# Retention and MLP on one core: splitting a mask, moving a cast, and swapping two loads in a queue

## The chip, the cores and the metric

The kernel runs on one core of one Trainium2 chip. The metric is the device time of one execution in microseconds (us), lower is better. Most executions of one kernel agree within about 0.3%, some 0.6 us here, and that turned out to be as large as everything that this change does. The chip's time is about 1.8 us longer than the span of the profile throughout: in the changed kernel, 215.22 us goes with a span of 213.4 us. Spans and moments inside the trace are used to find causes, repeated times to give verdicts.

## The reference, cut to what matters

A retention recurrence over 4 sequences of 768 steps with 8 heads of 64, then layer norm and an MLP of 512 to 2048 to 512 with a residual:

```python
for t in range(S):
    state = gamma * state + einsum('bhd,bhe->bhde', k[:, :, t], v[:, :, t])
    y[:, :, t] = scale * einsum('bhd,bhde->bhe', q[:, :, t], state)
...
x  = y, heads side by side: [4, 768, 512]
xn = (x - mean) / sqrt(var + 1e-6) * g_ln
out = x + relu(xn @ w_ch1) @ w_ch2
```

## The kernel before

The rows are cut into 24 tiles of 128. For each tile the recurrence is done in chunked form: k and q are transposed, for tiles 0 to 6 on TensorE (the code calls these steps tk and tq) and for later ones by DMA; the scores are a product `pa`, masked and evacuated to `asb` on VectorE, and the output `py` is `asb` by v plus q by the state. `pd` updates the state. Layer norm gives `xn`, which is transposed (tx; from tile 8 on by DMA), and the MLP follows. A unit of the first MLP matmul is 16 small matmuls: in the early groups, one tile by one quarter of `w1`, 0.89 us of TensorE. Up to a planned 14 us, gaps of TensorE are filled with matmuls of zeros, so not all of its busy time there is work.

The instruction order is not written by hand. Every step is a task with its durations, a rank and its inputs. A greedy planner simulates the engines and emits the tasks in the order that it finds:

```python
def order(self):
    ...
    while any(todo.values()):
        ...            # of all tasks that could start: the smallest (start + polite, rank, start)
        at = max(free[e], t["at"], ring[-self.depth] if t["load"] else 0)
        ...
        key = at + t["polite"], t["rank"], at
        if best is None or key < best[0]:
            best = key, t, e
```

So a changed constant of one task can move many others. The parts that the change touches are the mask of the scores, the casts of tile 0 (which alone arrives as fp32, by other queues), and the ranked list of loads that GpSimd issues:

```python
maskd = a(DVE, 1230, -50, c_mask, [vscd, tri])          # one 128 x 1024 product
...
loaded[kind, j] = a({"k": {ACT: 620}, "q": {DVE: 490}, "v": {ACT: 620, DVE: 430}}[kind], 0, -60, emit,
                    [raw], takes, [("osb", kind)])      # tile 0: v goes to either engine
...
first = ["iota", "pos", "k1", "q1", "v1", "w1_0", "k2", "q2", "w1_1", "v2", "k3", "q3", "v3",
         "w1_2", "k4", "q4", "v4", "w1_3", "k5", "q5", "v5"]
```

`w1_2` is the third of four quarters of the first weight, counted from 0. In the texts of the prediction and the experiments it is "quarter 3 of w1", and tiles are counted from 0.

## Time and profile before

| | before |
|---|---|
| time, median of 3 | 214.69 us (214.67 to 214.78) |
| span of the profiled execution | 213.1 us |
| TensorE busy | 203.6 us, 96% |
| first `pa` (scores of tile 0) starts | 7.69 us |
| first MLP unit starts | 13.69 us |
| k of tile 4 has landed, its transposes start | 23.34, 23.38 us |
| k of tile 6 has landed, its transposes start | 31.29, 32.75 us |
| second MLP matmul starts | 48.18 us |
| last matmul starts | 209.80 us |

Moments in tables and text are read from single records and can differ by 0.01 from the rows shown, by rounding. Reading it: TensorE has no long gap after the first 24 us, so the question for any early change is which of its early waits ends last. The prediction reads that out of the views. It does not show VectorE (DVE) at the head, which is what the change is about. In these rows of VectorE's timeline of the kernel before, the columns are start, duration, engine, line, operation, output and inputs, shapes, count, and in brackets the idle time ahead of the row with what ended it:

```profile
4.36 1.23 DVE L262 TENSOR_TENSOR mask<-vsc,cm 128x1024 f32<-128x1024 f32 x1
5.60 0.49 DVE L188 CAST qsb<-osb 128x512 bf16<-128x512 f32 x1
6.88 0.43 DVE L188 CAST v<-osb 128x512 bf16<-128x512 f32 x1 [0.79 <-DMA osb<-in_v_dram]
7.22 0.42 DVE L416 TENSOR_TENSOR trq<-tp,qsc 128x512 bf16<-128x512 bf16 x1
```

VectorE does the whole mask, casts q, then stands 0.79 us for the raw v, casts it, and only then scales the transposed q, on which the first `pa` waits. A chain of three small costs sits ahead of the first scores.

### The profile page before, as it was taken

How to read it: one execution, taken by the hardware profiler on the slowest of the kernel's cores; microseconds unless marked ns; L12 is line 12 of the kernel's file. 1: busy time of each engine (PE TensorE's matmuls, PEld its weight loads, DVE VectorE, ACT ScalarE, POOL GpSimd, SP SyncE). 2: the span in 40 equal slices, each digit the busy share in tenths (PEclk: the TensorE clock that was granted, in tenths of full speed). 3: DMA queues.
4: the chain of work that ended last, by engine and by line, in shares of the span. 5: the costliest groups of instructions: out<-in, count | busy, mean ns of one | idle time of the engine just before them, and what ended most of it. 6: DMA issues, size and time to landing. Idle time of an engine off the chain costs nothing.

```text
span 213.1 us, 4678 instructions
## 1 busy us (share of the span) xinstructions
PE 203.6 (96%) x1935; PEld 131.4 (62%) x1955; DVE 121.3 (57%) x235; ACT 80.8 (38%) x152; POOL 89.8 (42%) x105
## 2 busy tenths in 40 slices
PE   7769999999999999999999999999999999999994
PEld 2448899995476556777877785454544444444442
DVE  7688778961736989987872869793511111012121
ACT  4446655772042203645644353145640044430000
POOL 8988699826498395665834550000000000000000
PEclk9999999999999999999999999999999999999999
DMA  7999999999999999999999999820121111011212
GB/s 140 180 179 180 180 156 190 169 185 155 149 202 190 130 245 201 134 165 128 172 131 142 122 177 152 222 77 0 34 65 50 52 49 49 0 52 49 98 49 98
DMA packets 109382, 27.17 MB, mean 127 GB/s; under 512 B 102065, under 2 KB 106417, under 8 KB 109362
## 3 DMA queue, kind: packets, MB, share of 16 engines
q0 software_dynamic: 75984, 13.24, 87.8%
q1 hardware_dynamic: 32194, 13.31, 34.7%
q10 hardware_dynamic: 1184, 0.33, 0.7%
q8 instruction: 15, 0.25, 0.5%
q14 instruction: 5, 0.04, 0.1%
HBM read 27.27 MB, written 6.29 MB: 157 GB/s over the span
## 4 chain that ended last, share of the span: by engine, by line
PE 87%; DMA 8%; POOL 2%; issue 1%; DVE 0%; POOLq 0%
PE tp L626 39%; PE mm L589 37%; DMA ksb<-in_k_dram 5%; DMA w<-in_moe_w_ch_dram 3%; PE pa L443 3%; PE pd L512 2%; PE py L466 2%; PE py L462 2%; PE tp L542 1%; POOL k L342 0%; PE tp L403 0%; POOL qsb L342 0%; POOL v L342 0%; POOL w L350 0%; PE tp L411 0%
## 5 line engine op out<-in xcount | busy, mean ns | idle before, releaser
L589 PE MATMUL mm<-xnt,w 128*128 128x128 bf16 (+2 forms) x896 | 93.7, 257 | 0.0
L626 PE MATMUL tp<-w,h 128*128 128x512 bf16 (+2 forms) x381 | 86.7, 370 | 1.2 <-issue 0.3
L602 ACT ACTIVATE h<-mm 128x512 bf16<-128x512 f32 x88 | 52.5, 597 | 70.5 <-PE mm L589 59.6
L589 PEld LDWEIGHTS <-w 128*128 128x128 bf16 x896 | 65.7, 98 | 18.5
L626 PEld LDWEIGHTS <-h 128*128 128x128 bf16 x400 | 37.3, 98 | 38.8
L634 DVE SCALAR_TENSOR_TENSOR osb<-tp,rstd,x_all 128x512 f32<-128x512 f32 (+2 forms) x25 | 18.2, 728 | 55.3 <-PE tp L626 55.1
L450 DVE TENSOR_TENSOR asb<-pa,mask 128x1024 bf16<-128x1024 f32 x24 | 29.3, 1220 | 9.6 <-PE pa L443 9.4
L480 DVE BATCH_NORM_STATS2 bns<-py 128x6 f32<-128x512 f32 x24 | 16.7, 696 | 14.6 <-PE py L466 14.4
L499 POOL TENSOR_TENSOR vg<-vsb,vsc 128x512 bf16<-128x512 bf16 x16 | 17.2, 1073 | 13.3 <-DMA vsb<-in_v_dram 9.2
L486 ACT CAST x_all<-py 128x512 bf16<-128x512 f32 x24 | 14.0, 583 | 19.1 <-DVE xn L475 19.0
L342 POOL DMA_DIRECT2D qk<-in_k_dram x17 | 15.2, 893 | 12.3 <-DMA tr<-qk 9.9
L342 POOL DMA_DIRECT2D vsb<-in_v_dram x20 | 18.5, 923 | 1.2 <-DMA w<-in_moe_w_ch_dram 0.8
L475 DVE SCALAR_TENSOR_TENSOR xn<-py,mv,gb 128x512 bf16<-128x512 f32 x24 | 18.0, 751 | 0.9
L526 DVE TENSOR_TENSOR state<-pd,gch 64x256 bf16<-64x256 f32 x40 | 16.7, 417 | 0.3
L342 POOL DMA_DIRECT2D qk<-in_q_dram x17 | 15.2, 894 | 3.4 <-DMA w<-in_moe_w_ch_dram 3.4
L433 DVE TENSOR_TENSOR trq<-tr,qsc 128x512 bf16<-128x512 bf16 x17 | 7.9, 463 | 2.9 <-DMA tr<-qk 2.9
L564 ACT ACTIVATE rstd<-mv,epsb 128x1 f32<-128x1 f32 (+2 forms) x14 | 3.7, 289 | 11.8 <-DVE mv L481 11.8
L466 PEld LDWEIGHTS <-asb 128*128 128x128 bf16 x192 | 7.8, 98 | 0.3 <-DVE trq L416 0.3
L462 PEld LDWEIGHTS <-trq 128*128 128x128 bf16 x80 | 6.0, 98 | 3.2
L466 PE MATMUL py<-vsb,asb 128*128 128x64 bf16 x160 | 7.9, 193 | 0.0
L462 PE MATMUL py<-state,trq 128*128 128x128 bf16 x80 | 7.7, 219 | 0.1
L650 PE MATMUL mm<-zeros 128*128 128x512 bf16 (+1 forms) x24 | 6.4, 394 | 1.4 <-DVE zeros L221 1.2
(65 smaller groups left out, 108.4 us busy)
## 6 DMA issues: line engine op xcount, KB each, us to landing
out_dram<-osb SPq DMA_DIRECT2D x23, 256.0 KB, 4.0
w<-in_moe_w_ch_dram POOLq DMA_DIRECT2D x8, 512.0 KB, 10.3
vsb<-in_v_dram POOLq DMA_DIRECT2D x20, 128.0 KB, 8.8
qk<-in_k_dram POOLq DMA_DIRECT2D x17, 128.0 KB, 9.3
qk<-in_q_dram POOLq DMA_DIRECT2D x17, 128.0 KB, 9.9
qsb<-in_q_dram POOLq DMA_DIRECT2D x6, 128.0 KB, 8.7
k<-in_k_dram POOLq DMA_DIRECT2D x3, 128.0 KB, 7.4
v<-in_v_dram POOLq DMA_DIRECT2D x3, 128.0 KB, 9.0
```

The costliest lines, as they stand in the source:

```text
L342: nc.gpsimd.dma_start(out=tile_of(kind, j), in_=src)
L450: nc.vector.tensor_tensor(out=take("asb", t, [P, NPAIR, 2, P], BF16).rearrange("p i a t -> p a i t"), in0=held["pa", t], in1=mask.rearrang ...
L462: nc.tensor.matmul(py[:, 2 * i:2 * i + 2, :], lhsT=held["trq", t][:, i, :], rhs=held["pb", t][:, i, :], start=(mi == 0), stop=False)
L466: nc.tensor.matmul(py[:, h, :], lhsT=held["asb", t][:, h // 2, h % 2, :], rhs=tile_of("v", t)[:, h, :], start=(mi == 0), stop=(mi == n - 1))
L475: nc.vector.scalar_tensor_tensor(out=take("xn", t, [P, DM], BF16), in0=held["py", t].rearrange("p h d -> p (h d)"), scalar=mv[:, t, 0:1], ...
L480: nc.vector.bn_stats(out=bns[:, t, :], in_=held["py", t].rearrange("p h d -> p (h d)"))
L499: e.tensor_tensor(out=take("vg", j, [P, H, D], BF16), in0=tile_of("v", j), in1=vsc[:, cc, :].unsqueeze(2).to_broadcast([P, H, D]), op=ALU. ...
L526: nc.vector.tensor_tensor(out=held["pb", n][o, :, o], in0=held["pd", b][o, :, o], in1=gch[o, cc, :].unsqueeze(2).to_broadcast([D, NPAIR, D ...
L589: nc.tensor.matmul(p[:, j, :], lhsT=w1[:, ko, (ho + j) * P:(ho + j + 1) * P], rhs=held["xnt", hb][:, h0:h0 + n, ko, :], start=(ko == 0), s ...
L602: nc.scalar.activation(out=dst, in_=src, func=AF.Relu)
L626: nc.tensor.matmul(held[key], lhsT=held["h1", hb][:, ho, i * P:(i + 1) * P], rhs=w2[:, ho, cols], start=(ho == 0), stop=(ho == HO - 1))
L634: nc.vector.scalar_tensor_tensor(out=take("osb", key, [P, w], FP32), in0=held[key], scalar=rstd[:, t:t + 1], in1=x_all[:, t, cols], op0=AL ...
```

## The change

The intent is to start earlier: cut the mask in two so that half of it fills VectorE's idle time, give the cast of v to ScalarE, and put weights and v where the new, earlier TensorE order asks for them. Several cost constants of the planner are changed with it, so its whole early order shifts.

```diff
--- before.py
+++ after.py
@@ -258,10 +258,11 @@
         nc.vector.tensor_scalar(out=cm, in0=fidx, scalar1=pos[:, 0, 0:1], scalar2=None,
                                 op0=ALU.is_ge)
 
-    def c_mask(eng):
+    def c_mask(eng, s):
+        n = s.stop - s.start
         nc.vector.tensor_tensor(
-            out=mask, in0=vsc[:, 0, :].unsqueeze(2).to_broadcast([P, H, P]),
-            in1=cm.unsqueeze(1).to_broadcast([P, H, P]), op=ALU.mult)
+            out=mask[:, s], in0=vsc[:, 0, s].unsqueeze(2).to_broadcast([P, n, P]),
+            in1=cm.unsqueeze(1).to_broadcast([P, n, P]), op=ALU.mult)
 
     def c_gch(eng):
         for c in range(1, C):
@@ -272,7 +273,7 @@
             nc.gpsimd.memset(x, 0.0)
 
     a = plan.add
-    small = a(DVE, 1450, -100, c_small)
+    small = a(DVE, 1550, -100, c_small)
     small2 = a(DVE, 200, -99, c_small2)
     iota = a(POOL, 250, 0, c_iota)
     ipos = a(POOL, 250, 0, c_pos)
@@ -285,7 +286,9 @@
     table = a(ACT, 1300, -100, lambda eng: None)
     vscd = a(ACT, 250, -90, c_vsc, [lmul, table])
     qscd = a(ACT, 700, -91, c_qsc, [args, table])
-    maskd = a(DVE, 1230, -50, c_mask, [vscd, tri])
+
+    maskd = a(DVE, 640, -50, lambda eng: c_mask(eng, slice(0, H // 2)), [vscd, tri])
+    maskd = a(DVE, 640, -45, lambda eng: c_mask(eng, slice(H // 2, H)), [maskd], at=5300)
     gchd = a(ACT, 900, 100, c_gch, [small, qscd, vscd], at=9000)
     zerod = a(POOL, 500, 0, c_zero, at=9000)
     exps = [gchd, qscd, vscd]
@@ -327,12 +330,12 @@
                     dst = take("osb", kind, [P, DM], FP32).rearrange("p (h d) -> p h d", d=D)
                     (nc.scalar if eng == ACT else nc.sync).dma_start(out=dst, in_=src)
                 raw = a(ACT if kind == "q" else SP, 390, -200 + "kqv".index(kind), emit32, (),
-                        ("osb", kind), (), 0, {"k": 3400, "q": 4000, "v": 4800}[kind])
+                        ("osb", kind), (), 0, {"k": 3400, "q": 3800, "v": 5200}[kind])
 
                 def emit(eng):
                     evacuate(eng, take(*takes, [P, H, D], BF16),
                              held["osb", kind].rearrange("p (h d) -> p h d", d=D))
-                loaded[kind, j] = a({"k": {ACT: 620}, "q": {DVE: 490}, "v": {ACT: 620, DVE: 430}}[kind], 0, -60, emit,
+                loaded[kind, j] = a({"k": {ACT: 620}, "q": {DVE: 490}, "v": {ACT: 620}}[kind], 0, -60, emit,
                                     [raw], takes, [("osb", kind)])
                 return
 
@@ -349,15 +352,15 @@
             def emit(eng):
                 nc.gpsimd.dma_start(out=dst, in_=src)
         loaded[kind, j] = a(POOL, ns, rank, emit, (), takes, uses, dma,
-                            4000 if kind in "qkv" and j > 7 else 1400 if late(kind, j) else 500,
+                            4000 if kind in "qkv" and j > 7 else 1400 if late(kind, j) else 900 if kind == "w1" and j else 500,
                             follows=follows)
 
     def late(kind, j):
-        return j > 2 if kind in "qkv" else kind == "w2" or j > 0
-
-
-    first = ["iota", "pos", "k1", "q1", "v1", "w1_0", "k2", "q2", "w1_1", "v2", "k3", "q3", "v3",
-             "w1_2", "k4", "q4", "v4", "w1_3", "k5", "q5", "v5"]
+        return j > 2 if kind in "qkv" else kind == "w2" or j > 1
+
+
+    first = ["iota", "pos", "k1", "q1", "v1", "w1_0", "k2", "q2", "w1_1", "v2", "k3", "q3", "w1_2",
+             "v3", "k4", "v4", "q4", "w1_3", "k5", "v5", "q5"]
     pool_rank = {x: i - 1000 for i, x in enumerate(first)}
     seq = [(x, t) for t in range(8) for x in "kqv"] + [("w1", j) for j in range(4)]
     seq += [("w2", j) for j in range(4)] + [(x, 8) for x in "kqv"]
@@ -516,7 +519,7 @@
                 pdt = a(PE, 230, r - 1 if cc == 0 else r + 2.2, e_pd,
                         [vgt, loaded["k", j]] + ([pbt[j]] if cc else []),
                         ("pd", b) if cc == 0 else None,
-                        [("vg", j), where["k", j]] + ([("pd", b)] if cc else []), at=0 if cc or b else 20000)
+                        [("vg", j), where["k", j]] + ([("pd", b)] if cc else []), at=0 if cc or b else 19000)
 
                 def e_pb(eng, n=number[b, cc + 1], b=b, cc=cc):
```

> **What bounds the kernel now.** I first read the page's busy line and its chain of shares. They say that TensorE (PE) is the bound, with one stretch of DMA in the chain.
>
> ```profile
> PE 203.6 (96%) x1935; PEld 131.4 (62%) x1955; DVE 121.3 (57%) x235; ACT 80.8 (38%) x152; POOL 89.8 (42%) x105
> PE 87%; DMA 8%; POOL 2%; issue 1%; DVE 0%; POOLq 0%
> ```
>
> The busy line hides when PE is free, so I read the waits of PE next. Each row is who waited for whom, total us, times, longest.
>
> ```profile
> PE pa L443 <- DVE trq L416: 1.1, 2, 0.6
> PE mm L542 <- DVE xn L475: 0.7, 1, 0.7
> PE tp L542 <- DVE xn L475: 0.7, 1, 0.7
> ...
> PE tp L403 <- DMA ksb<-in_k_dram: 0.4, 1, 0.4
> ```
>
> There are few, and the timeline dates them: 12.18, 15.76, 20.42 us and, last of all, 23.39 us. The chain that ended last, asked for the first 30 us in order of time (start, us, what), shows what that last one is.
>
> ```profile
> 4.19 7.25 DMA w<-in_moe_w_ch_dram
> 11.45 0.28 issue
> 11.73 0.76 POOL w L350
> 12.49 0.17 issue
> 12.66 10.68 DMA ksb<-in_k_dram
> 23.34 0.05 issue
> 23.39 0.40 PE tp L403 x4
> 23.78 0.89 PE mm L589 x16
> 24.68 0.22 PE tp L411 x4
> 24.90 0.89 PE mm L589 x16
> ```
>
> The reader is to see a hand-over. Up to 23.34 us the end is set by a load: k of tile 4, issued at 12.66 and landed 10.68 us later, because it stands in a queue of loads. From 23.39 us on there is only PE, back to back, to the end of the span (213.1 us). So the time is **the start of the transposes of k of tile 4, plus 189.7 us of PE work** (213.1 - 23.39). Gaps of PE before 23.39 us cost nothing by themselves: whatever PE gains there, it waits away at that load.
>
> The timeline of PE around that point shows how the wait is filled today:
>
> ```profile
> 20.42 0.40 PE L443 MATMUL pa<-trq,trk 64*128 64x128 bf16 x8 [0.44 <-DVE trq L416]
> 20.75 1.96 PE L589 MATMUL mm<-xnt,w 128*128 128x128 bf16 x32
> 22.55 0.40 PE L466 MATMUL py<-v,asb 128*128 128x64 bf16 x8
> 23.39 0.40 PE L403 MATMUL tp<-idn,ksb 128*128 128x128 bf16 x4 [0.44 <-DMA ksb<-in_k_dram]
> ```
>
> The x32 are two units of the first MLP matmul (16 matmuls = one tile by one quarter of w1, 0.89 us). By the program's order they are tile 2 by quarters 1 and 2, which are on the chip long before.
>
> **What the Trainium skill says.** "TensorE: Matmul & The Clock Gate", section Back-to-back issue gap, gives N/2.4 + 2.5 ns for an isolated warm matmul, 55.8 ns at N = 128. The trace agrees: 0.89 us for 16. This pitch is what makes 189.7 us a constant. The same page, section What's actually happening, says that the PE clock halves after an idle window of about 3.4 us; the longest gap here is under 1 us, and I expect one of 1.2 us, so no clock loss. "DMA: Bandwidth & Descriptors", section Why a DMA increments its semaphore by 16 and not by 1: only the sixteenth engine's increment means landed. The trace agrees and it matters: v of tile 3 landed on the median engine at 18.80 us and on the last at 20.11. "Runtime: NRT & Kernel Launch", section Instruction fetch mechanics: instructions come in blocks of 16 KiB by DMA. The trace has 15 packets of 16384 bytes on an instruction queue, the first at 17.81 us for 1.06 us; from there on the last engine trails the median by about 1.2 us instead of 0.4.
>
> **The change, part by part.**
>
> Early part (mask in two runs, v of tile 0 on ScalarE). The cast of q waits for its raw load, which the DMA semaphore has at 5.58 us, and it started at 5.60 us; the first mask half now ends near 5.0, so the cast still starts at 5.60. The second half then takes about 0.64 us (half of 1.23, rounded up) from 6.0 to 6.65. Before, VectorE waited there for the raw v (landed 6.86), cast it (6.88 to 7.31), and only then scaled q at 7.22. Now q is scaled at about 6.6. The first pa goes from 7.69 to about 7.07, bounded also by the k evacuation at 6.62. That 0.62 us is carried: the asb product ends near 8.74 instead of 9.36, xn of tile 0 near 11.48 instead of 12.12, and the first MLP matmuls start at about 13.0 instead of 13.70. ScalarE takes the 0.62 us cast at 6.88, where it idled 1.84 us. All of this is ahead of 23.39 us and is worth **0** by the hand-over.
>
> Load order. Software loads wait for the eighth before them, as the program's waits say. Numbering them, k of tile 4 is the 13th before and after, with the same loads ahead of it: v of tile 3 and quarter 3 of w1 only swap places 11 and 12. The swap doesn't change when k is issued: in both orders the 12th waits for quarter 1 of w1 (11.45), so k still goes at about 12.6. The DMA row of the page is at 9 tenths there, so no starving. **k of tile 4 lands at 23.3 us as before.**
>
> What the new PE order puts before those transposes. Counting in both orders: the same four pairs of transposes, four pa and py, three xn transposes, one pd, six MLP units. The work left is the same 189.7 us. But the last two units ahead of py of tile 3 are now tiles 0 and 1 by **quarter 3 of w1**, no longer tile 2 by quarters 1 and 2. So PE waits for that quarter. Its landing: the load ahead of it, q of tile 3, was last to land at 18.51 us. Quarter 3 takes 2.34 to 2.41 us (20.11 to 22.45 on the last engine, 18.80 to 21.21 on the median). The instruction fetch adds 0.7 to 0.9 to the slowest engine. That is 21.55 to 21.8, I take 21.65. PE reaches that point near 20.4 (pa of tile 3 at about 20.0 against 20.42), so it idles about 1.25 us. Then 1.79 us for the two units, 0.23 for py of tile 3 (its v lands near 22.5, in time), and the transposes of k start at 21.65 + 0.05 + 1.79 + 0.23 = 23.72, after its landing at 23.34. Net: **+0.33 us** against 23.39.
>
> After it. q of tile 4 now lands in place 15, 24.95 us; its transposes come after k's and two units, at about 25.7, so no wait. xn of tile 3: py at 23.5, plus 0.43, 0.95 and 0.75 from the timeline's spacings, is 25.65, needed near 25.95. k of tile 6 (place 20, 31.29) is needed near 31.6. Margins are 0.3 us each: thin, but positive. Sum: 214.69 + 0.33 = **215.0 us**.
>
> **The rivals.**
>
> (a) The gain at the head comes through: 0.6 to 1.0 us less, 213.7 to 214.1. For it: two VectorE waits really shrink, and the change looks aimed at them. Against: the landing of k of tile 4 would have to move with them, and nothing ahead of it in the queue gets shorter.
>
> (b) The landing of quarter 3 is 0.4 us earlier than I work out (the fetch falls on another load or engine): then both waits coincide and the time is 214.7. If the fetch's delay went away altogether, k itself would land near 22.5 and the time would be near 214.0. I hold this unlikely, since the fetch comes with PE's place in its instruction stream, which hardly moves.
>
> (c) A later wait opens, because xn of tile 3 or k of tile 6 misses its 0.3 us margin, or quarter 4 (27.53, needed near 28.4): 0.2 to 0.6 more, 215.2 to 215.6.
>
> (d) The reordering after 60 us costs or gives: PE showed no wait for 189.7 us there and the counts are equal, so within 0.1 us.
>
> **Range and chances.** The sum's own spread is the landing of quarter 3, about 0.2 us either way; (b) pulls to 214.5, (c) to 215.5. I take 214.5 to 215.5. A change of 2% is 4.3 us, more than all of PE's idle time in the waits, so within 2% is nearly certain.
>
> **What would show it.** Right: in the chain, the hand-over from DMA to PE is at quarter 3 of w1, and PE shows a wait of over 1 us for that load near 20.4 us; the first pa is near 7.1 us; k's transposes start near 23.7 us with no wait for k. Wrong: the hand-over is earlier than 23.3 us, k of tile 4 lands earlier than 23.0, or PE waits for anything after 24 us.

## The result

| | time, median | lowest to highest | runs |
|---|---|---|---|
| before | 214.74 us | 214.67 to 214.97 | 4 |
| after | 215.1 us | 214.86 to 215.22 | 4 |
| after, a second time, other chip | 215.1 us | 214.97 to 215.19 | 6 |
| before, beside that | 214.88 us | 214.52 to 215.47 | 11 |

The ratio is 1.0014 (95% interval 0.9996 to 1.0031) the first time and 1.0007 (0.9994 to 1.0021) the second: the same time within 2%, and not even a loss of 0.1% is proven. A ratio is the mean time of one kernel's fast runs over that of the other's fast runs of the same rounds, so it is not quite the ratio of the medians quoted. All runs of this table's kernel after were fast ones at a granted clock of 0.998 to 1.0.

At the head the change does what it was made for. VectorE and ScalarE (ACT) in the timeline of the kernel after:

```profile
5.38 0.71 DVE L188 CAST qsb<-osb 128x512 bf16<-128x512 f32 x1 [0.33 <-DMA osb<-in_q_dram]
6.01 0.67 DVE L263 TENSOR_TENSOR mask<-vsc,cm 128x512 f32<-128x512 f32 x1
6.65 0.42 DVE L419 TENSOR_TENSOR trq<-tp,qsc 128x512 bf16<-128x512 bf16 x1
6.70 0.62 ACT L188 CAST v<-osb 128x512 bf16<-128x512 f32 x1 [0.29 <-DMA osb<-in_v_dram]
```

The half mask takes the place of the wait for v, q is scaled at 6.65 in place of 7.22 us, and v is cast beside it. The first `pa` moves from 7.69 to 7.12 us, the first MLP unit from 13.69 to 12.91 us. By 20 us TensorE is still 0.38 us ahead (`pa` of tile 3 at 20.04 against 20.42). Then the timeline of TensorE after shows where that goes:

```profile
20.04 0.40 PE L446 MATMUL pa<-trq,trk 64*128 64x128 bf16 x8
21.19 1.96 PE L592 MATMUL mm<-xnt,w 128*128 128x128 bf16 x32 [0.75 <-DMA w<-in_moe_w_ch_dram]
22.98 0.40 PE L469 MATMUL py<-v,asb 128*128 128x64 bf16 x8
23.21 0.39 PE L406 MATMUL tp<-idn,ksb 128*128 128x128 bf16 x4
```

The wait of 0.44 us for k of tile 4 is gone, and a wait of 0.75 us for a quarter of w1 stands in its place, two rows earlier. The transposes of k of tile 4 start at 23.21 us, 0.17 us earlier than before. Yet the span is 0.3 us longer. The chain that ended last, after (start, duration, what):

```profile
10.02 11.12 DMA w<-in_moe_w_ch_dram
...
22.38 8.94 DMA ksb<-in_k_dram
31.32 0.05 issue
31.36 0.40 PE tp L406 x4
```

In this execution the hand-over from loads to TensorE is not at 21.19 us but a whole load later: k of tile 6 was issued at 22.38, behind a load of q that had itself waited for the w1 quarter to land, and landed at 31.32. Without waits TensorE would have taken it up at about 31.02 us. It lost 0.09 us at the `pd` of tile 5 just before, for GpSimd's scaling of v (done at 30.84 us), and waited the other 0.25 us for the load, because the changed order wants k of tile 6 earlier: 7.82 us after k of tile 4 without waits, against 9.37 us before. The second execution shows the other case. There the w1 quarter landed later, 21.40 us, and the chain goes straight from it to TensorE:

```profile
10.02 11.38 DMA w<-in_moe_w_ch_dram
21.40 0.05 issue
21.45 1.96 PE mm L592 x32
...
23.64 0.22 PE tp L406 x4
```

The account of the two executions against the kernel before, in starts of matmuls:

| term | before | after | difference | second after | difference |
|---|---|---|---|---|---|
| transposes of k of tile 4 | 23.38 | 23.21 | -0.17 | 23.47 | +0.09 |
| from there to the second MLP matmul | 24.80 | 25.13 | +0.33 | 24.83 | +0.03 |
| from there to the last matmul | 161.62 | 161.80 | +0.18 | 161.63 | +0.01 |
| last matmul | 209.80 | 210.15 | +0.35 (terms +0.34) | 209.94 | +0.14 (terms +0.13) |

The third term is probably not the change's: a second trace of the kernel before has 161.78 there, with the same instructions. By the single records, nearly all of it is one wait of 0.16 us, near 132 us in that trace and near 117.5 us in the first trace after: one VectorE product, the scaling of a later tile's transposed q (`trq`), took 0.90 and 0.99 us there in place of 0.41. What lengthens it in some executions is not known.

### The profile page after: what moved, and what is told of

It is laid out like the page before. It is cut to its first block, busy times and chain, and to the rows that moved or that the text cites. A ratio compares the mean times of both kernels' runs of the same rounds, so it can differ in the third digit from the quotient of the medians.

```text
span 213.4 us, 4674 instructions
## 1 busy us (share of the span) xinstructions
PE 203.8 (95%) x1932; PEld 131.7 (62%) x1955; DVE 121.8 (57%) x234; ACT 82.5 (39%) x154; POOL 89.2 (42%) x105
## 4 chain that ended last, share of the span: by engine, by line
PE 82%; DMA 9%; POOL 5%; DVE 1%; issue 1%; POOLq 0%
PE tp L629 38%; PE mm L592 34%; DMA w<-in_moe_w_ch_dram 5%; DMA ksb<-in_k_dram 4%; PE pa L446 3%; PE py L469 2%; PE py L465 2%; PE pd L515 2%; POOL qsb L345 2%; POOL k L345 1%; POOL v L345 1%; POOL w L353 1%; DVE trq L436 0%; PE tp L545 0%; DVE xn L478 0%
## 5 line engine op out<-in xcount | busy, mean ns | idle before, releaser
L489 ACT CAST x_all<-py 128x512 bf16<-128x512 f32 x24 | 14.0, 584 | 17.9 <-DVE xn L478 17.8
L436 DVE TENSOR_TENSOR trq<-tr,qsc 128x512 bf16<-128x512 bf16 x17 | 9.0, 527 | 3.0 <-DMA tr<-qk 2.8
```

## The experiments

Moving one constant makes the planner reorder everything. So in each experiment the planner of one of the two kernels runs unchanged, and single tasks are then moved in the list that it returns; every other order on every engine is kept. A line such as `move(out, A, B)` below means "emit A right after B"; `("e_m1", ("1", 2, 12))` is the MLP unit of tile 2 by quarter 4 (12/4 = 3, counted from 0). All results were correct; every timed run counts as a fast one, but for the single run of before_again, which has no state. Ratios are to the kernel before, in the same rounds.

| run | base | edit | median us | ratio (95%) | span | k of tile 4 starts | second MLP starts |
|---|---|---|---|---|---|---|---|
| after_again | after | none | 215.1 | 1.0007 (0.9994 to 1.0021) | 213.2 | 23.47 | 48.30 |
| before_again | before | none | 215.0 (one run) | | 213.2 | 23.35 | 48.15 |
| head_alone | before | early part | 214.66 | 0.9994 (0.9979 to 1.0009) | 212.9 | 23.19 | 47.99 |
| swap_alone | before | two loads swapped | 214.98 | 1.0009 (0.9993 to 1.0024) | 213.7 | 23.55 | 48.34 |
| swap_undone | after | swap taken back | 216.73 | 1.0103 (1.0061 to 1.0145) | 214.3 | 24.56 | 49.35 |
| k4_late | before | k of tile 4 two places later | 216.65 | 1.0083 (1.0068 to 1.0098) | 214.6 | 24.91 | 49.71 |
| k6_later | after | k of tile 6 one unit later | 215.17 | 1.0026 (1.0000 to 1.0052) | 215.0, half clock | 25.22 | 50.07 |
| fill_best | after | 20 to 36 us reordered | 215.45 | 1.0026 (1.0014 to 1.0038) | 213.5 | 23.70, one unit more done | 48.57 |
| fill_act | fill_best | 3 relu to ScalarE | 214.89 | 1.0002 (0.9990 to 1.0014) | 212.9 | 23.66, one unit more done | 48.20 |
| head_fill | head_alone | unit ahead of k of tile 4 | 214.46 | 0.9983 (0.9969 to 0.9998) | 212.9 | 23.53, one unit more done | 47.97 |
| head_fill_act | head_fill | 3 relu to ScalarE | 214.32 | 0.9980 (0.9966 to 0.9993) | 212.5 | 23.19, one unit more done | 47.54 |
| head_fill_q5 | head_fill_act | unit ahead of q of tile 5 | 214.52 | 0.9994 (0.9981 to 1.0008) | 212.6 | 23.51, one unit more done | 47.65 |

### Each part alone, and a known dose

**after_again**, the changed kernel once more beside the experiments on it.

> The changed kernel once more, for a second trace and a ratio over more rounds. Hand-over theory (the end is set by the last load that PE waits for, plus PE work): about 0.2 to 0.5 us over the kernel before; the third quarter of w1 lands between 21.0 and 21.8 us, and PE waits again at the transposes of k of tile 6, whose load lands at 31.2 to 31.5 us. Noise theory (the two kernels are equal): within 0.1 us, and no wait at k of tile 6.

Measured: 215.1 us and the second execution of the account above: w1 quarter at 21.40, no wait of more than 0.03 us after 24 us.

**head_alone**, the early part without the rest.

```diff
+ half = [{**maskd, "emit": lambda eng, s=s: c_mask(eng, s)} for s in (slice(0, H // 2), slice(H // 2, H))]
+ out[i] = half[0]                        # in the place of the whole mask
+ out.insert(after_the_cast_of_q, half[1])
+ loaded["v", 0]["eng"] = ACT
+ move(out, ("load", "v", 0), ("e_ek", 0))
```

> The kernel before with the head part alone (mask in two runs, v of tile 0 cast by ScalarE), all loads and the order of PE as before. Hand-over theory: the first pa starts near 7.1 us instead of 7.7, and the time is that of the kernel before within 0.2 us, since PE waits for k of tile 4 at 23.3 us as before, only longer. Rival (the head's gain counts, and the load order takes it away again): 0.6 to 1.0 us faster than before.

Measured: the first `pa` starts at 7.12 us, 0.57 earlier, and the time is 214.66 us against 214.88 in the same rounds, an interval that holds 1. TensorE's timeline has the reason:

```profile
20.36 0.40 PE L444 MATMUL pa<-trq,trk 64*128 64x128 bf16 x8 [0.44 <-DVE trq L417]
...
23.20 0.40 PE L404 MATMUL tp<-idn,ksb 128*128 128x128 bf16 x4 [0.31 <-DMA ksb<-in_k_dram]
```

With the old order the 0.57 us are gone by 20.36 us (20.42 before), and what decides is again k of tile 4, which in this execution landed at 23.15 in place of 23.34. The 0.2 us of the span is that landing, not the head.

**swap_alone**, the two loads swapped in the kernel before.

```diff
+ move(out, ("load", "v", 3), ("load", "w1", 2))
```

> The kernel before with one move: the third quarter of w1 is loaded ahead of v of tile 3, every engine's order kept. Hand-over theory: v of tile 3 lands near 22.3 us, just ahead of the asb product that its py needs (22.4), and k of tile 4 lands at 23.3 as before: the time of the kernel before within 0.2 us. Rival (the swap of the loads is what costs): 0.3 us or more slower.

Measured: 214.98 us, ratio 1.0009 with an interval that holds 1. k of tile 4 landed at 23.50, later by 0.16 in this one trace, which is within the spread between executions (22.85 to 23.50 in the traces where it stands 13th). Swapping two loads ahead of it does not move it by more.

**swap_undone**, the changed kernel with the loads as they were.

```diff
+ move(out, ("load", "w1", 2), ("load", "v", 3))
```

> The changed kernel, its order on PE, VectorE and ScalarE kept, with v of tile 3 loaded ahead of the third quarter of w1 again. Hand-over theory: that quarter lands 0.9 to 1.0 us later (near 22.1), the transposes of k of tile 4 start near 24.2, the wait at k of tile 6 goes away (0.3 us), so 0.6 to 0.7 us slower than the changed kernel, about 215.7. Rival (the load order is what costs): at the changed kernel's time or faster.

Measured: the direction as the hand-over theory says, by more than it says. The quarter landed at 22.49 us (expected near 22.1) and tk of tile 4 started at 24.56 us (expected near 24.2), 1.09 later than in after_again; k of tile 6 is not waited for, and the span is 1.1 us longer. Only half of the runs tell that cleanly: three took 215.83 to 216.07 us at full clock, three took 217.4, 217.67 and 218.87 at a mean clock of 0.992, 0.992 and 0.982. The wait that the swap avoids is in TensorE's timeline, 1.62 us where the changed kernel has 0.67 to 0.75:

```profile
22.54 1.96 PE L592 MATMUL mm<-xnt,w 128*128 128x128 bf16 x32 [1.62 <-DMA w<-in_moe_w_ch_dram]
```

So the change's own order needs this swap: the reordering alone would cost 1.1 us and the clock besides, the swap gives it back, and the two together come out near zero.

**k4_late**, a dose: k of tile 4 loaded two places later in the kernel before.

```diff
+ move(out, ("load", "k", 4), ("load", "v", 4))
```

> The kernel before with k of tile 4 loaded after q and v of tile 4, every engine's order kept: a dose for the hand-over. Hand-over theory: k of tile 4 lands 1.6 to 1.8 us later, near 25.0, and the whole time grows by as much, to about 216.3. Rival (the loads lie beside other work and PE is the bound by itself): no change.

Measured: k landed at 24.86 us, 1.52 later than before (23.34; 1.6 to 1.8 was expected), and its wait grew:

```profile
24.91 0.40 PE L403 MATMUL tp<-idn,ksb 128*128 128x128 bf16 x4 [1.76 <-DMA ksb<-in_k_dram]
```

The start moved by 1.53 us, the second MLP matmul by 1.53, the span by 1.5 and the time by 1.8 (216.65 against 214.88). From the hand-over to the second MLP matmul it is 24.80 us, to the hundredth as before. This confirms the hand-over in the kernel before: whatever delays that landing delays the end as much.

**before_again**, one look at the kernel before.

> The kernel before once more, for the spread of landings between traces. Hand-over theory: k of tile 4 lands between 22.9 and 23.5 us, PE waits for it, and the span is 189.7 us after the start of its transposes, within 0.1 us.

Measured as expected: landing 23.30, start 23.35, and a span of 213.2.

### The wait behind, and a clock that halves

**k6_later**, the changed kernel with the transposes of k of tile 6 behind one more MLP unit, to take the 0.34 us wait away.

```diff
+ move(out, ("e_tk", 6), ("e_m1", ("1", 2, 12)))
```

> The changed kernel with one move on PE: the transposes of k of tile 6 after the next unit of 16 MLP matmuls instead of before it. Hand-over theory: the wait of about 0.25 us at 31.1 us goes away and the time falls by 0.2 to 0.3 us against the changed kernel, to that of the kernel before or 0.1 us above. If that wait is not on the path: no change against the changed kernel.

Measured: a miss. The five runs at full clock gave 214.93 to 215.92 us, no better than the changed kernel. after_again suggests why: with the w1 quarter landing at 21.40 or later, k of tile 6 is waited for by only 0.03 us, so there is nothing to take away. No trace of k6_later at full clock shows it. The sixth run, the profiled one, took 216.75 us. In stretches of 2 us, its busy times and granted clock (PEclk, third from the end of the row) are:

```profile
20.00:22.00 2.00, 1.04 (x19) 0.78 (x17) 1.95 (x4) 0.75 (x2) 1.00 (x2) 0.99 2.34 157
22.00:24.00 2.00, 2.00 (x22) 2.00 (x20) 0.31 (x1) 0.60 (x1) 1.63 (x2) 0.50 2.09 173
```

TensorE was busy 1.04 of 2 us in the first row (the figure after the length; 1.35 in the 2 us before that), no single gap longer than 0.89 us, and then the clock was at half from 21.95 us for 3.41 us: two MLP units took 3.35 in place of 1.96 us. The same must lie behind the slow half of swap_undone, by the arithmetic: 3.41 us at half clock is 1.7 of 215 us, a mean clock of 0.992. That is argued, not shown, for the runs that have no trace.

### Can the waits be filled?

If the hand-over is all, then putting an MLP unit into the wait should move the end by the wait. Four kernels try it.

**fill_best**: the changed kernel with its TensorE, VectorE and ScalarE order between 20 and 36 us rearranged by hand, so that one more unit stands ahead of k of tile 4 and k of tile 6 is asked for later.

```diff
+ want = [("e_am", 3), ("load", "q", 5), ("e_m1", ("1", 2, 0)), ..., ("e_py", 3), ("e_bn", 3),
+         ("e_m1", ("1", 1, 8)), ..., ("e_tk", 4), ..., ("e_tk", 6), ..., ("e_py", 5)]   # cut
+ out = [t for t in out if t not in took]; out[at[0]:at[0]] = took
```

> The changed kernel, its loads and head kept, with the order on PE, VectorE and ScalarE from 20 to 36 us set by when the loads were seen to land: MLP units whose data is there go ahead of k of tile 4, of q of tile 5 and of k of tile 6. Hand-over theory: PE waits nowhere over 0.4 us after 20 us, and the time is 0.6 to 0.9 us under the changed kernel, about 214.2 to 214.5, that is 0.3 to 0.6 under the kernel before. Rival (the changed kernel is at the end of what order can give): no gain against the kernel before.

Measured: a miss, 215.45 us, slower than before by 0.26% with an interval clear of 1. k of tile 4 was asked for at 23.70 us with one more unit (0.89 us) done, so TensorE was 0.57 us ahead of the kernel before (23.38 - 22.81); at the second MLP matmul it was 0.39 us behind.

**fill_act**: the same, and three relu evacuations (the relu that empties an MLP unit's result buffer) on ScalarE in place of VectorE.

```diff
+ for x in [(2, 4), (2, 12), (4, 4)]:
+     relu[x]["eng"] = ACT
```

> Edit: as the rearranged changed kernel (fill_best, 215.45), and three relu evacuations (tile 2 quarters 2 and 4, tile 4 quarter 2) on ScalarE in place of VectorE. If VectorE took back what that order gained: 0.4 to 0.7 us less than 215.45, so 214.7 to 215.0. If not: 215.3 to 215.6.

Measured: 214.89 us, 0.56 less than fill_best, as expected of VectorE as the second bound. The two ran on different chips, and their ratios (1.0026 and 1.0002) have intervals that touch at 1.0014, so the traces carry it. Busy times in stretches of 6 us (TensorE, weight load, VectorE, ScalarE, GpSimd), fill_best and then fill_act:

```profile
32.00:38.00 6.00, 5.58 (x104) 5.07 (x102) 4.92 (x10) 2.76 (x6) 6.00 (x8) 1.00 1.59 190
38.00:44.00 6.00, 5.96 (x107) 5.75 (x108) 5.53 (x13) 4.89 (x11) 4.02 (x5) 1.00 1.24 189
```
```profile
32.00:38.00 6.00, 5.58 (x104) 5.07 (x102) 4.24 (x9) 3.27 (x7) 6.00 (x8) 1.00 1.59 193
38.00:44.00 6.00, 6.00 (x113) 6.00 (x114) 5.55 (x12) 5.39 (x12) 3.98 (x5) 1.00 1.23 189
```

VectorE gave 0.68 us away between 32 and 38 us, and TensorE got six more matmuls done in the 6 us after: in the records of single matmuls, two stops of 0.14 and 0.20 us ahead of MLP matmuls, at 40.6 and 42.8 us, are there in fill_best and gone in fill_act. By their semaphores, a relu on VectorE ended both: MLP units waited for a result buffer that VectorE had yet to empty. Of the 0.96 us that fill_best lost between k of tile 4 and the second MLP matmul (24.87 us against 23.91 = 24.80 - 0.89), fill_act got back 0.33. The idle time of TensorE between 32 and 38 us (6.00 - 5.58 = 0.42 us) stayed, 0.17 us of it for `trk` from ScalarE and 0.24 us for `xn` from VectorE, so this relief was only a part.

**head_fill**: the early part alone, plus an MLP unit by the w1 quarter ahead of k of tile 4 and one more ahead of q of tile 4.

```diff
+ move(out, ("e_tk", 4), ("e_m1", ("1", 0, 8)))
+ move(out, ("e_tq", 4), ("e_m1", ("1", 1, 8)))
```

> Edit: the kernel before with only the early part of the change (mask in two runs, v of tile 0 on ScalarE), and on TensorE the transposes of k of tile 4 moved behind the MLP unit of tile 0 by quarter 3 of w1, and those of q of tile 4 behind the next unit, so that the wait for k of tile 4 is filled. Loads and every other order kept. Theory (hand-over at k of tile 4, nothing behind it near): quarter 3 lands at 22.2 to 22.5, so TensorE runs that unit from 22.5 and the end moves 0.4 to 0.6 us earlier than in the early part alone: a span near 212.4, a time near 214.2. Rival (VectorE and the later loads are a second bound just behind): the start of the second MLP matmul moves by less than 0.2 us, the time stays at 214.6 to 214.9, and new waits on VectorE appear between 30 and 48 us.

Measured: 214.46 us, ratio 0.9983, but on the trace neither theory's path. The wait for k of tile 4 is gone, and TensorE was 0.55 us ahead (22.64 + 0.89 = 23.53, where head_alone would be at 24.08). Then the chain:

```profile
19.05 10.55 DMA qsb<-in_q_dram
29.61 0.05 issue
29.65 0.40 PE tp L412 x4
```

q of tile 5 landed at 29.61 us and TensorE waited 0.30 us for it. In head_alone it landed at 29.38 and its transposes start at 29.68 with no wait: this load had 0.30 us of slack, and came 0.23 us later in this execution. Before that, TensorE had waited 0.19 us for quarter 4 of w1, which landed at 27.73 us. The second MLP matmul starts at 47.97 us against 47.99. Not VectorE but the next two loads in the queue took the gain back. It is a third possibility that I had put into one clause of the rival and given no number.

**head_fill_act**: three relu evacuations on ScalarE besides.

```diff
+ for x in [(1, 8), (2, 12), (4, 4)]:
+     relu[x]["eng"] = ACT
```

> Edit: as head_fill, and three of the relu evacuations between 30 and 45 us (tile 1 quarter 3, tile 2 quarter 4, tile 4 quarter 2) on ScalarE in place of VectorE. If VectorE is the second bound: 0.2 to 0.4 us less than head_fill and the second MLP matmul starts at 47.5 or earlier. If it is not: equal to head_fill within 0.1 us, or slower, should ScalarE's queue make the transposes wait.

Measured: 214.32 us, ratio 0.9980. Its trace ends 0.4 us earlier than head_fill's, but not through the relu: q of tile 5 landed 0.44 us earlier in this execution (29.17), and from its transposes to the second MLP matmul it is 18.32 us in both traces. So VectorE is not the bound in this order, against what fill_best seemed to promise. The queue of loads was simply earlier in this run, from its first weight on (10.96 against 11.34 us).

**head_fill_q5**: one more unit, put into the wait for q of tile 5.

```diff
+ move(out, ("e_tq", 5), ("e_m1", ("1", 1, 12)))
```

> Edit: as head_fill_act, and the transposes of q of tile 5 moved behind the next MLP unit (tile 1 by quarter 4 of w1). In head_fill and head_fill_act TensorE ran 0.5 us ahead until it waited 0.45 us for q of tile 5 (landed 29.61 and 29.17), and everything after it moved with that landing. If that load was the whole of the second bound: the second MLP matmul starts 18.3 - 0.4 us after its landing in place of 18.3, the span is 0.3 to 0.45 us less at equal landings (about 212.1 to 212.5), the time 213.9 to 214.2 (ratio to the kernel before near 0.9965). Rival: the evacuations on VectorE and ScalarE between 32 and 44 us take it back, with new waits of TensorE on xn or trq; the time stays at 214.3 to 214.5.

Measured: by its trace the wait for q of tile 5 is gone and the second MLP matmul starts at 47.65 us, 0.34 earlier than in head_alone with k of tile 4 landing within 0.06 us of it. Less than the 0.57 us that were there to win (23.19 against 23.51 - 0.89), because a further holder comes up: `pd` of tile 4 now waits 0.20 us for GpSimd (POOL), which scales v of tile 4 only after two load issues. The 0.45 us of the expectation was too much besides: by the records, TensorE waited 0.30 us for q of tile 5 in head_fill and 0.25 in head_fill_act. GpSimd's row and TensorE's:

```profile
25.54 1.06 POOL L500 TENSOR_TENSOR vg<-vsb,vsc 128x512 bf16<-128x512 bf16 x1
```
```profile
26.65 0.38 PE L513 MATMUL pd<-vg,ksb 128*128 128x128 bf16 x4
```

By repeated times it is 214.52 us, ratio 0.9994, an interval that holds 1: the gain seen in one trace is not confirmed, and the expected 213.9 to 214.2 was missed. Three versions that fill the waits lie at 0.9980 to 0.9994 of the kernel before. head_fill and head_fill_act have intervals just below 1, so a version some 0.2% (0.4 us) faster than both kernels seems to exist; which of the three is best, these runs can't tell.

## Why the prediction was right, and where its working was not

**The number and the class held.** Predicted 215.0 us in a range of 214.5 to 215.5; measured 215.1 twice. Within 2% as said. But the range holds the time before too, and the two ratios hold 1, so the time alone does not tell the sum of +0.33 us from no change at all; what tests the steps is the traces and the runs with one part moved.

**The hand-over at k of tile 4** as the bound of the kernel before held exactly: a dose of 1.52 us in its landing gave 1.53 us at its start (k4_late).

**The early part worth nothing** held. The first `pa` was expected at 7.07 and came at 7.12 us; the first MLP unit was expected at 13.0 and came at 12.91 and 13.04. Alone, it changed the time by less than the spread (head_alone).

**k of tile 4 landing as before**: predicted 23.3, measured 23.05 and 23.30, and never waited for in the changed kernel.

**The new wait for the w1 quarter** was the right mechanism with a wrong size. The landing was worked out as 21.65 us; it was 21.14 and 21.40. The wait was to be 1.25 us ("over 1 us" among the signs); it was 0.75 and 0.67. The failed term is the landing: the sum started from q of tile 3 at 18.51 and added the weight's 2.4 us and the instruction block's delay on top. In the first trace q of tile 3 itself landed at 18.01 (0.25 us of the difference was there from the first weight on, 11.20 against 11.45), and 3.13 us later the weight, which fits the sum's 2.4 + 0.73 but from the earlier start. In the second, q of tile 3 landed at 19.42, and only 1.98 us later the weight: the last engine was already behind when it took the weight up.

The block came at 17.3 us, in place of 17.8 before, just as q of tile 3 was landing (17.83 and 17.90 on the median engine), so I read it as having fallen on that load in the second trace; the records do not say which engine carried it, and in the first trace, with the block at 17.32, that load was not late. The prediction had said that PE's place in its instruction stream "hardly moves". The block moved by 0.5 us, and not simply with the head's gain: it came at 17.39 and 17.40 us in swap_alone and k4_late, which do not have that gain, and at 17.89 in head_alone, which has it. Nor is the late load the change's alone: q of tile 3 landed at 19.17 to 19.57 us in seven of the nine traces with the block at 17.41 or earlier, those two among them, and by 18.54 in all five with a later block. What moves the block stays open. The late q of tile 3 also cost TensorE 0.55 us in the second trace, so its `pa` of tile 3 came at 20.38 and the shorter weight wait is no gain. So k of tile 4 started at 23.21 and 23.47, not at 23.72.

**"After it" missed, by margins.** k of tile 6 was to have 0.3 us in hand. With TensorE 0.51 us earlier than predicted in the first trace, the margin was used up and became a loss of 0.34 us: the start of rival (c), and the sign "PE waits for anything after 24 us" that the prediction itself named as proof of a wrong step. In the second trace it was 0.03. The two errors offset each other, and not by luck alone: k of tile 6, landing near 31.3 us in every trace of either kernel, stands 7.82 us behind k of tile 4 in the new order, and so holds the end as if k of tile 4 started no earlier than 31.36 - 7.82 = 23.54. An earlier w1 quarter could not have been worth anything. This is also why rival (b), 214.7 us if both waits coincide, did not come: its premise came true in the first trace, its time did not.

**Rivals.** (a), the head's gain coming through, fell by head_alone and by the result. (d), the order after 60 us, shows 161.80 and 161.63 against 161.62 and 161.78 before: no effect that can be told from the spread.

**The clock reading** (gaps too short for a loss) held in both traces of the changed kernel, with a gap left out: the list of waits, of which the prediction shows a part, opens with one of 1.2 us at the start of the program. It is no safe rule, as k6_later lost its clock after gaps of at most 0.89 us.

What stays open: whether the true difference is 0 or +0.3 us. The medians say +0.2 to +0.4, the intervals allow none.

## What to carry to other kernels

A gain ahead of a load that stands in a queue is worth nothing until the load moves, so first ask which wait ends last, and then which load lies next behind it: here k of tile 6, quarter 4 of w1, q of tile 5 and GpSimd's scaling of v each held TensorE once it ran no more than 0.6 us ahead, in one order or another, and each filled wait uncovered another. When one edit makes a planner reorder everything, freeze the order and move single tasks: it showed that the reordering cost 1.1 us and the swapped load paid it back, which the total hides. Where landings vary by 0.2 to 0.5 us between executions, a margin of 0.3 us is not a margin, and one trace does not prove a gain of that size.

## What the Trainium skill lacked or had wrong

- "TensorE: Matmul & The Clock Gate", section What's actually happening, and its advice to avoid idle gaps of more than about 3 us: here the clock fell to half for 3.41 us after gaps of at most 0.65 and 0.89 us, with TensorE busy 1.35 and 1.04 of 2 us in the stretches ahead of it, and in other executions it stayed full after gaps of 1.62 us (swap_undone) and 1.76 us (k4_late). In the 3.41 us before the clock fell TensorE was busy 1.81 us; in k4_late it was busy only 1.70 of the 3.42 us up to 24.87 us, and the clock stayed full. So scattered idle time of half such a stretch can be enough, in some executions only, and what decides is not shown. The length of the slow stretch agrees with the page.
- The same page, section Back-to-back issue gap, gives about 81 ns at N = 128 and 131 ns at N = 512 for matmuls sustained in real kernels. This kernel sustains 0.89 us for 16, that is 56 ns, at N = 128 and 216 ns at N = 512, with a weight load before each: in both cases what the page calls the isolated figure.
- "Runtime: NRT & Kernel Launch", section Instruction fetch mechanics, calls the fetch of the 16 KiB blocks hidden behind the issue of the engine that runs them. It does not say that a block, the first one a single packet of 0.99 to 1.06 us here, can hold up data loads. That it does is read from the timing, not tested: the last engine trailed the median by 0.2 to 0.5 us before the first block and by 0.9 to 1.3 us after it (v of tile 3, quarter 3 of w1 and k of tile 4 in the kernels before and after).
